# Turning the token rows of a mixture-of-experts kernel: from TensorE transposes to VectorE block transposes, with plain reads two groups ahead

## The chip, the core and the metric

The kernel runs on one core of a Trainium2 chip, in one launch. The metric is device time in microseconds, the median of several runs. The engines have these names in the profile: PE (TensorE, matrix products), PEld (its weight loads), DVE (VectorE), ACT (ScalarE), POOL (GpSimd), SP (SyncE, which here only issues DMA transfers). Data that the engines work on lies in SBUF, 128 partitions wide; matrix products are written to PSUM.

## The reference

Linear attention without a softmax, an RMS norm, then a mixture of experts in which each token goes to one expert.

```python
# q, k, v: (8, 8, 576, 64) float32;  g_norm: (64,)
kv  = np.einsum('bhsd,bhse->bhde', k, v)
out = np.einsum('bhsd,bhde->bhse', q, kv)
rms = np.sqrt(np.mean(out * out, axis=-1, keepdims=True) + 1e-06)
x   = (out / rms * g_norm)         # -> (4608 tokens, 512), heads side by side
# w_gate: (512, 8), w1: (8, 512, 1024), w2: (8, 1024, 512)
logits     = x @ w_gate
expert_idx = argmax(logits);  gate_w = softmax(logits)[expert_idx]
for e in range(8):
    mask = expert_idx == e
    out[mask] = gate_w[mask, None] * (np.maximum(x[mask] @ w1[e], 0) @ w2[e])
```

## The kernel before

It has two phases that overlap a little. In the attention phase, for each of 8 batches, it loads q, k, v, forms `kv`, and makes for each tile of 128 tokens the normalised row (`xrow`, 512 values of 16 bits, without the factor `g_norm`, with the gate weight and the number of the token behind it: 516 words of 16 bits, 1032 bytes) and the logits. Rows go to a table in DRAM, `x_slots`, in which expert e owns the rows from e * 4608 on; a running count gives each token its place. The writes are indirect DMA from POOL, one for each tile of 128 tokens.

```python
# inside the attention phase
xrow[j, t // 3] = PA.tile([128, 3, ROW], I16, tag="xrow", bufs=4, ...)     # three tiles to a buffer
...
def o_x(j, t):                                        # DVE: row and logits, scaled by 1/rms
    nc.vector.tensor_tensor(xr[:, 0:D]..., xv, _bc(rs2, 3, 64), op=ALU.mult)
    nc.vector.tensor_tensor(lhat[j][:, t]..., lv, _bc(rs2, 3, 8), op=ALU.mult)
...
chunks = {0: [(0, 9)], 1: [(0, 9)], 2: [(0, 3), (3, 9)], 3: [(0, 3), (3, 6), (6, 9)]}   # tiles routed together
...
for t in range(T):                                    # end of route(): scatter the rows
    nc.gpsimd.indirect_dma_start(out=xs_views[9 * j + t0 + t], out_offset=...posi..., in_=xrow[...])
```

The expert phase works through 11 groups: the first three 128-row tiles of experts 0, 1 and 2 ("early" groups, whose rows are complete before the last batches are routed), then the two remaining tiles of each of these, then experts 3 to 7 with five tiles each. A small group for tiles beyond five ("spill") stands before the last. A group reads its rows by indirect DMA on POOL (`fetch`), one for each tile; rows that hold no token are left out by the bounds check, over a buffer cleared at the start. PE turns each tile with four transposes, DVE brings the result to SBUF and multiplies by `g_norm`; `stage1` is the first product with ReLU on ACT, `stage2` the second, with the gate weight on DVE and an indirect DMA of the result rows.

```python
xl_ring = [P_const.tile([128, SLOT_TILES, ROW], I16, ...) for n in range(3)]
...
def fetch(self):                      # POOL, one for each tile k
    nc.gpsimd.indirect_dma_start(out=self.xl[:, k, :], in_=xs.ap(), in_offset=...idx...,
                                 bounds_check=E * N - 1, oob_is_err=False)
def xpose(self, k):
    ps = PSA.tile([128, 4, 128], F16, tag="KV", bufs=2, name="xps")
    for c in range(4):
        nc.tensor.transpose(ps[:, c, :], self.xl[:, k, c * 128 : (c + 1) * 128].bitcast(F16), ident16)
    nc.vector.tensor_scalar(self.xsT[:, :, k * 128 : (k + 1) * 128], ps, g2, None, op0=ALU.mult)
def stage1(self, f):                  # f = 0..7; two column halves for groups of five tiles
    for kk in range(4):
        for hp, s in zip(hps, starts):
            nc.tensor.matmul(hp, self.w()[0][:, kk, f * 128 : (f + 1) * 128],
                             self.xsT[:, kk, s : s + self.step], ...)
    nc.scalar.activation(self.hT[:, f, ...], hp, ACTF.Relu)
def stage2(self, k):
    for f in range(8):
        nc.tensor.matmul(yp, self.hT[:, f, k * 128 : (k + 1) * 128], self.w()[1][:, f, :], ...)
    nc.vector.tensor_scalar(y, yp, self.xl[:, k, D : D + 2].bitcast(F32), None, op0=ALU.mult)
    nc.gpsimd.indirect_dma_start(out=self.views(k), out_offset=...ids..., in_=y, ...)
```

The groups' order of work is a generator, `ffn()`, whose units are called by the end of the attention phase and then to the end. While group n is in `stage2`, the tiles of group n+1 are turned; `fetch` of group n+2 is issued after the first unit of group n. The weights come from SP as float32 pieces of 512 KB into four staging buffers (`wst`); `w_step` casts the oldest to float16 on DVE and loads one more. The tables for the spill group (`dyn_tables`) are some 35 small DVE operations that run in one go inside the first two-tile group. At the very end every engine loads the number of further spill tiles (`n_more`) into a register, and a loop, usually of no turns, follows.

Of the kernel before, what the change touches and what calls it, by code (L numbers as in the profile page):

```python
# [45 lines left out]
def kernel(  # L46
# [20 lines left out]
    xs_views = dram_disjoint_views(xs.ap(), NT)  # L67
# [9 lines left out]
    for j in range(4):  # L77
# [20 lines left out]
        "w1off": arf[:, None] + 128.0 * np.array([0, 2, 1, 3], np.float32)[None, :],  # L98
# [36 lines left out]
    nc.scalar.dma_start(g2[64:128, :], g_norm.unsqueeze(1))  # L135
    wgt = P_const.tile([128, 8, 8], F32, tag="wgt")
# [17 lines left out]
    chunks = {0: [(0, 9)], 1: [(0, 9)], 2: [(0, 3), (3, 9)], 3: [(0, 3), (3, 6), (6, 9)]}  # L154
    ohbs, n_route = [], 0
    for j in range(4):
# [7 lines left out]
    xl_ring = [  # L164
        P_const.tile([128, SLOT_TILES, ROW], I16, tag=f"xl{n}", name=f"xl{n}") for n in range(3)
    ]
# [7 lines left out]
    w_tiles = {}  # L174

# [4 lines left out]
    def w_load(pool, bufs):  # L180
# [23 lines left out]
        if n < 4:  # L204
            r0 = 128 * (2 * (n % 2) + n // 2)
            nc.sync.dma_start(st, w1[r0 : r0 + 128, :])
# [8 lines left out]
        w_staged.append((e, dst, st))  # L215

    def w_cast(engine):
        if w_staged:
            e, dst, st = w_staged.pop(0)
            engine.tensor_copy(dst, st)  # L220
            w_done[e] = w_done.get(e, 0) + 1
# [4 lines left out]
    def w_step():  # L226
        if len(w_staged) == 4 or not w_todo:
            w_cast(nc.vector)
# [8 lines left out]
    cnt = P_const.tile([128, 8], F32, tag="cnt")  # L237
    srow = P_const.tile([128, 8, SLOT_TILES], F32, tag="srow")
# [4 lines left out]
    def row_index(name, ctr, ne, nk):  # L243
        bad = P_const.tile([128, ne, nk], F32, tag="bad" + name, name="bad" + name)
        nc.vector.tensor_tensor(
            bad, _bc(cv["srank"][:, 0:nk], 1, ne), _bc(ctr[:, 0:ne], 2, nk), op=ALU.is_ge
        )
        idx = P_const.tile([128, ne, nk], I32, tag="idx" + name, name="idx" + name)
        nc.vector.scalar_tensor_tensor(
            out=idx, in0=bad, scalar=BIG, in1=srow[:, 0:ne, 0:nk], op0=ALU.mult, op1=ALU.add  # L250
        )
        badi = P_const.tile([128, ne, nk], I32, tag="badi" + name, name="badi" + name)
        nc.vector.tensor_scalar(badi, bad, BIG, None, op0=ALU.mult)
        return idx, badi

    rows = {}

    def early_rows():
        ctr = P_const.tile([128, 8], F32, tag="cnt_e")
        b0 = base[len(routed)]  # L260
        nc.vector.tensor_tensor(ctr, b0, cv["ebase"], op=ALU.subtract)
        rows["early"] = row_index("e", ctr, EARLY, EARLY_TILES)
        nc.vector.tensor_tensor(b0, b0, cv["efloor"], op=ALU.max)
        yield
        for i in range(EARLY):
            groups[i].fetch()
        yield

    def final_rows():
        nc.vector.tensor_tensor(cnt, base[n_route], cv["ebase"], op=ALU.subtract)  # L270
        rows["all"] = row_index("a", cnt, 8, SLOT_TILES)

    class Group:
        def __init__(self, n, e, k0, k1):
# [4 lines left out]
            self.xl = xl_ring[n % 3]  # L279
            self.table = "early" if self.small and k0 == 0 else "all"  # L280

# [6 lines left out]
        def fetch(self):  # L288
            idx = rows[self.table][0]
            for k in range(self.K):  # L290
                nc.gpsimd.indirect_dma_start(  # L291
                    out=self.xl[:, k, :], out_offset=None, in_=xs.ap(),
                    in_offset=IndirectOffsetOnAxis(
                        ap=idx[:, self.e, self.k0 + k : self.k0 + k + 1], axis=0
                    ),
                    bounds_check=E * N - 1, oob_is_err=False,
                )

        def slot_ids(self):
            badi = rows[self.table][1]  # L300
# [3 lines left out]
                self.xl[:, 0 : self.K, D + 2 : D + 4].bitcast(I32),  # L304
                badi[:, self.e, self.k0 : self.k0 + self.K].unsqueeze(2), op=ALU.max,
            )

# [6 lines left out]
        def start(self):  # L314
            self.xsT = self.pool().tile(
# [577 lines left out]
```

## Time and profile before

| quantity | before |
|---|---|
| time, median of 3 runs (lowest to highest) | 330.64 us (329.99 to 332.32) |
| span of the profiled execution | 329.2 us |
| PE busy | 269.0 us, 82% |
| DVE busy | 183.4 us, 56% |
| ACT busy | 119.9 us, 36% |
| POOL busy | 137.6 us, 42% |
| DMA | 85.79 MB, mean 261 GB/s |
| PE transposes of rows (`xps`) | 160 and 4 for the spill tile, 16.1 us busy |
| their evictions on DVE (`xsT`) | 41, 19.2 us busy, 477 ns each |
| reads of rows on POOL (`xl`) | 40, 42.3 us busy |
| PE idle before matmuls of attention for DVE's `lhat` | 9.6 us in 3 waits |

The profile is one execution. Busy times of engines overlap, so they do not add up to the span; what counts is which engine is waited for at a given moment. Its second part cuts the span into 40 equal slices and gives busy tenths, so that phases can be told apart; PEclk is the clock that PE was granted, in tenths of full speed. The chain of waits follows the work that ended last back in time. In the timeline, a line is: start, length, engine, line of the source, operation, output and input, count, and in brackets the idle time ahead of it with what ended it.

### The profile page before, as it was taken

The page shows a single profiled execution, that of the slowest core. Times are in us where ns is not written, and L with a number is a line of the kernel's source. Part 1 is how long each engine was busy: PE and PEld are TensorE (multiplying, and loading weights), DVE is VectorE, ACT ScalarE, POOL GpSimd, SP SyncE. Part 2 cuts the span into 40 slices and gives each one's busy share as a digit, 9 for nine tenths or more (in the row PEclk, how much of TensorE's full clock was granted, in tenths as well). Part 3 has the DMA queues.
Part 4 walks back from the last instruction along what each step waited for, and adds up shares of the span by engine and source line. Part 5 has one row for each costly group of instructions (what it writes and reads, how often), then busy time and mean ns, then how long its engine had stood idle before and what let it go on. Part 6 is the DMA issues. An engine that isn't in the chain of part 4 may idle for free.

```text
span 329.2 us, 7247 instructions
## 1 busy us (share of the span) xinstructions
PE 269.0 (82%) x2759; PEld 189.3 (58%) x2759; DVE 183.4 (56%) x433; ACT 119.9 (36%) x316; POOL 137.6 (42%) x147
## 2 busy tenths in 40 slices
PE   0699897689766977564979996989999999997980
PEld 0587776577656866462535563657565665645630
DVE  6205566346745368889184678344657658375040
ACT  1136564436543445322322431326142240602600
POOL 9100001720076004384675462777477656052041
PEclk9999997959995589555999998999999999999996
DMA  6999999997897016799589894667799999983021
GB/s 158 334 368 367 369 368 367 381 282 216 246 323 295 18 67 167 250 323 324 201 260 372 295 322 121 214 214 251 250 339 358 351 397 279 408 284 130 0 99 55
DMA packets 45395, 85.79 MB, mean 261 GB/s; under 512 B 6188, under 2 KB 22829, under 8 KB 45360
## 3 DMA queue, kind: packets, MB, share of 16 engines
q1 hardware_dynamic: 36736, 66.07, 59.9%
q0 software_dynamic: 6976, 18.96, 15.6%
q10 hardware_dynamic: 1648, 0.29, 0.5%
q8 instruction: 22, 0.36, 0.4%
q14 instruction: 13, 0.11, 0.1%
HBM read 71.77 MB, written 15.50 MB: 265 GB/s over the span
## 4 chain that ended last, share of the span: by engine, by line
PE 26%; issue 11%; DMA 9%; POOL 7%; DVE 5%; POOLq 1%; ACT 0%; DVEq 0%; ACTq 0%
PE hp L345 13%; PE yp L361 11%; DMA out_dram<-y,d_id 7%; POOL out_dram L369 4%; POOL xl L291 2%; DMA xl<-x_slots,idxe 2%; PE xps L325 1%; DVE y L366 1%; DMA x_slots<-xrow,posi 1%; POOL x_slots L743 1%; DVE w1e L220 1%; DVE xsT L328 0%; POOLq L888 0%; POOLq L854 0%; DVE w2e L220 0%
## 5 line engine op out<-in xcount | busy, mean ns | idle before, releaser
L353 ACT ACTIVATE hT<-hp 128x320 f16<-128x320 f32 (+3 forms) x136 | 53.6, 426 | 106.5 <-PE hp L345 105.9
L345 PE MATMUL hp<-xsT,w1e 128*128 128x320 f16 (+2 forms) x512 | 76.6, 306 | 7.2 <-DVE xsT L328 6.3
L361 PE MATMUL yp<-w2e,hT 128*128 128x512 f16 x320 | 74.1, 379 | 0.3 <-DVE y L366 0.3
L369 POOL DMA_INDIRECT out_dram<-y,idv x40 | 44.6, 1115 | 60.3 <-DVE y L366 49.3
L345 PEld LDWEIGHTS <-w1e 128*128 128x128 f16 x512 | 51.0, 100 | 32.1 <-issue 11.7
L651 PE MATMUL ops<-kvx,qT 64*128 64x72 f32 (+1 forms) x640 | 48.0, 310 | 10.5 <-DVE lhat L680 9.6
L743 POOL DMA_INDIRECT x_slots<-xrow,posi x36 | 35.7, 991 | 40.5 <-DVE xrow L739 15.5
L651 PEld LDWEIGHTS ops<-kvx,qT 64*128 64x128 f32 (+1 forms) x640 | 42.3, 215 | 15.0 <-issue 9.3
L361 PEld LDWEIGHTS <-hT 128*128 128x128 f16 x328 | 30.8, 98 | 31.6 <-issue 0.4
L366 DVE TENSOR_SCALAR y<-yp,xl 128x512 f32<-128x512 f32 x40 | 30.0, 750 | 33.6 <-PE yp L361 29.9
L664 DVE TENSOR_REDUCE ms<-sq 128x8 f32<-128x512 f32 x36 | 24.6, 685 | 25.1 <-ACT sq L660 25.0
L291 POOL DMA_INDIRECT xl<-x_slots,idxa x31 | 32.4, 1046 | 11.7 <-issue 7.0
L594 PE MATMUL kvps<-mk,mv 128*64 128x64 f32 x640 | 28.7, 258 | 9.4 <-DMA mv<-in_v_dram 9.1
L676 DVE TENSOR_TENSOR xrow<-ops,rs 128x512 f16<-128x512 f32 x36 | 24.7, 686 | 18.0 <-DMA x_slots<-xrow,posi 9.3
L660 ACT ACTIVATE sq<-ops 128x512 f32<-128x512 f32 x36 | 21.5, 598 | 31.9 <-PE ops L651 31.5
L594 PEld LDWEIGHTS kvps<-mk,mv 128*64 128x64 f32 x640 | 26.0, 168 | 11.8 <-issue 10.3
L710 POOL COPY xrow<-tokc 128x3 int32<-128x3 int32 x12 | 3.0, 253 | 64.3 <-DVE xrow L676 64.2
L582 PE MATMUL tps<-ctile,mq 128*128 128x128 f32 x144 | 26.9, 320 | 3.5 <-ACT qT L583 1.9
L220 DVE CAST w2e<-wst 128x1024 f16<-128x1024 f32 x32 | 22.3, 704 | 11.4 <-DMA wst<-in_moe_w_dram 11.4
L583 ACT COPY qT<-tps 128x384 f32<-128x384 f32 x48 | 21.9, 473 | 14.4 <-PE tps L582 14.4
L328 DVE TENSOR_SCALAR xsT<-xps,g 128x512 f16<-128x512 f16 x41 | 19.2, 477 | 12.9 <-PE xps L325 12.7
L220 DVE CAST w1e<-wst 128x1024 f16<-128x1024 f32 x32 | 21.6, 688 | 4.5 <-DMA wst<-in_moe_w_dram 4.5
(99 smaller groups left out, 184.1 us busy)
## 6 DMA issues: line engine op xcount, KB each, us to landing
wst<-in_moe_w_dram SPq DMA_DIRECT2D x64, 512.0 KB, 5.8
mq<-in_q_dram SPq DMA_DIRECT2D x16, 576.0 KB, 7.8
mk<-in_k_dram SPq DMA_DIRECT2D x16, 320.0 KB, 7.5
mv<-in_v_dram SPq DMA_DIRECT2D x16, 320.0 KB, 7.3
mk<-in_k_dram SPq DMA_DIRECT2D x16, 256.0 KB, 7.9
mv<-in_v_dram SPq DMA_DIRECT2D x16, 256.0 KB, 7.1
wsts<-in_moe_w_dram SPq DMA_DIRECT2D x8, 512.0 KB, 5.9
out_dram<-y,idv POOLq DMA_INDIRECT x40, 4.9
```

Of the source, the lines that this page charges most:

```text
L220: engine.tensor_copy(dst, st)
L291: nc.gpsimd.indirect_dma_start(out=self.xl[:, k, :], out_offset=None, in_=xs.ap(), in_offset=IndirectOffsetOnAxis(ap=idx[:, self.e, self.k ...
L345: nc.tensor.matmul(hp, self.w()[0][:, kk, f * 128 : (f + 1) * 128], self.xsT[:, kk, s : s + self.step], start=(kk == 0), stop=(kk == 3),)
L353: nc.scalar.activation(self.hT[:, f, s : s + self.step], hp, ACTF.Relu)
L361: nc.tensor.matmul(yp, self.hT[:, f, k * 128 : (k + 1) * 128], self.w()[1][:, f, :], start=(f == 0), stop=(f == 7),)
L366: nc.vector.tensor_scalar(y, yp, self.xl[:, k, D : D + 2].bitcast(F32), None, op0=ALU.mult)
L369: nc.gpsimd.indirect_dma_start(out=self.views(k), out_offset=IndirectOffsetOnAxis(ap=self.ids[:, k : k + 1], axis=0), in_=y, in_offset=Non ...
L582: nc.tensor.transpose(ps[:, c, :], src[:, 128 * m : 128 * m + 128], cv["ident"])
L594: nc.tensor.matmul(kvps[b][64 * y : 64 * y + 64, 2 * u + a, :], main["v", b, u][:, 2 * y + a, c, :], main["k", b, u][:, 2 * y + a, c, :], ...
L651: nc.tensor.matmul(ps[p0 : p0 + 64 * n, y, o0 : o0 + 72], qT[b][hs, a, blk // 2 : blk // 2 + n, :].rearrange("d c p -> d (c p)"), kvx[b][h ...
L676: nc.vector.tensor_tensor(xr[:, 0:D].bitcast(F16).rearrange("p (a h d) -> p a h d", a=2, h=4), xv, _bc(rs2, 3, 64), op=ALU.mult,)
L743: nc.gpsimd.indirect_dma_start(out=xs_views[9 * j + t0 + t], out_offset=IndirectOffsetOnAxis(ap=posi[:, t : t + 1], axis=0), in_=xrow[j, ( ...
```

## The change

Rows are now turned by DVE in blocks of 32 x 32. To make a 128-wide turn out of such blocks, a group's rows are read by four plain DMAs from SP, each with one quarter of the columns (128 of 512) of all rows of the group into 32 partitions; a block of 32 rows then lies across 32 partitions, and DVE's transpose puts the columns where the product wants them. The columns come out in the order p * 4 + c, so the first weight matrix is read in rows of that order, and `g_norm` (as `g4`) moves into the cast of the weights. Gate weight and token number come by a fifth small DMA (`gi`).

Plain reads take all rows, those without a token too, so these must hold zeros: for the early groups the slots are cleared by a DMA from a zero tile before any row is written (`clear_early`); for the others, POOL writes zero rows into the empty slots only (`pads`), by indirect DMA. Reads are issued two groups ahead, paddings three; the turn of group n+1 stands within `stage1` of group n. Beside this: six `xrow` buffers in place of four, other chunks for batch pair 2, casts shared between DVE and ACT in the last batches, one copy moved from DVE to ACT, more units of the expert phase within the last batch, the tables spread over units, the register load of `n_more` moved into the middle of the expert phase, and other PSUM tags for some tiles.

```diff
+    zero = P_wa.tile([128, F], F32, tag="wst", bufs=4, name="zero")
+    nc.gpsimd.memset(zero[:, 0 : EARLY_TILES * ROW // 2], 0.0)
+    def clear_early(e):
+        nc.sync.dma_start(xs.ap()[e * N : e * N + 128 * EARLY_TILES]..., zero[...].bitcast(I16))
...
         def fetch(self):
-            idx = rows[self.table][0]
-            for k in range(self.K):
-                nc.gpsimd.indirect_dma_start(out=self.xl[:, k, :], ... in_=xs.ap(), ...)
+            r0 = self.e * N + 128 * self.k0
+            src = xs.ap()[r0 : r0 + self.n].rearrange("(g b) w -> b g w", b=32)
+            self.xl = self.pool().tile([128, self.n // 32, 128], I16, tag="xl", bufs=2, name="xl")
+            for i in range(4):
+                c0 = 128 * (2 * (i % 2) + i // 2)
+                nc.sync.dma_start(self.xl[32 * i : 32 * i + 32], src[:, :, c0 : c0 + 128])
+            self.gi = P_fe.tile([128, SLOT_TILES, 4], I16, tag="gi", bufs=3, name="gi")
+            nc.sync.dma_start(self.gi[:, 0 : self.K], xs.ap()[r0 : r0 + self.n, D:ROW]...)
...
+        def pads(self):
+            for k in range(self.K):
+                nc.gpsimd.indirect_dma_start(out=self.pad_views[k], out_offset=...pad..., in_=zrow, ...)
...
-        def xpose(self, k): ...four PE transposes and an eviction with g2...
+        def xpose(self, part=0, parts=1):
+            gs = slice(g * part // parts, g * (part + 1) // parts)
+            nc.vector.transpose(self.xT[:, gs], self.xl[:, gs].rearrange("p g (a c) -> p g c a", c=4))
...
             for f in range(8):
                 cur.stage1(f)
+                if f == 0 and real >= 0:
+                    fetch_up_to(real + 2)
+                    if EARLY - 1 <= real < len(groups) - 3:
+                        groups[real + 3].pads()
                 if f % 2 == 1 if cur.K != 2 else f % 4 == 1:
                     w_step()
-                if f == 0 and 1 <= real and EARLY <= real + 2 < len(groups):
-                    groups[real + 2].fetch()
+                if f >= 4 and f % 2 == 0 and (f - 4) // 2 < parts:
+                    nxt.xpose((f - 4) // 2, parts)
...
-                    [128, 3, ROW], I16, tag="xrow", bufs=4, name=f"xrow{j}{t}"
+                    [128, 3, ROW], I16, tag="xrow", bufs=6, name=f"xrow{j}{t}"
...
-            nc.vector.tensor_copy(kvx[b][:, 1], folds[b][1])
+            nc.scalar.copy(kvx[b][:, 1], folds[b][1])
...
-                for _ in range((0, 1, 1, 2)[max(b - 5, 0)]):
-                    w_step()
-                if b == B and n >= 3:
+                if b == 6 and n >= 1:
+                    w_load(P_wa, 3)
+                elif b == 7:
+                    w_step(nc.vector if n % 2 else nc.scalar)
+                elif b == B:
+                    w_step()
+                    w_step(nc.scalar)
+                if b == B and n >= 1:
                     unit()
                     unit()
```

## The prediction

> **What bounds the kernel now.** First the page's forty slices, where the two phases show.
>
> ```profile
> PE   0699897689766977564979996989999999997980
> ...
> DVE  6205566346745368889184678344657658375040
> ...
> PEclk9999997959995589555999998999999999999996
> DMA  6999999997897016799589894667799999983021
> ```
>
> A slice is 8.2 us. Up to slice 10 DMA is full (q, k, v): attention is paced by its inputs. In slices 12 to 18 (99 to 156 us) DMA falls away, PE holds 4 to 9 tenths at half clock, DVE 7 to 9: attention's tail and the routing. From slice 19 PE is at 9: the expert phase, PE-bound. So two questions: what holds up the middle, and what PE does in the last 160 us.
>
> For the middle I read the timelines of DVE and PE, then windows of 3 us (columns: PE, PEld, DVE, ACT, POOL busy us; clock, DMA share, GB/s).
>
> ```profile
> 100.33 0.69 DVE L676 TENSOR_TENSOR xrow<-ops,rs 128x512 f16<-128x512 f32 x1 [5.01 <-DMA x_slots<-xrow,posi]
> ```
> ```profile
> 67.34 1.98 PE L651 MATMUL ops<-kvx,qT 64*128 64x72 f32 x16 [3.90 <-DVE lhat L680]
> ...
> 101.26 1.98 PE L651 MATMUL ops<-kvx,qT 64*128 64x72 f32 x16 [3.21 <-DVE lhat L680]
> ...
> 118.45 1.11 PE L651 MATMUL ops<-kvx,qT 64*128 64x72 f32 x16
> ```
> ```profile
> 97.00:100.00 3.00, 0.58 (x3) 0.31 (x3) 0.00 (x0) 0.41 (x2) 2.12 (x3) 0.64 1.03 400
> 100.00:103.00 3.00, 1.74 (x16) 1.75 (x16) 2.56 (x11) 0.88 (x3) 1.16 (x2) 0.50 1.03 402
> ...
> 115.00:118.00 3.00, 3.00 (x46) 2.87 (x46) 1.69 (x4) 0.92 (x3) 0.00 (x0) 0.50 0.00 0
> 118.00:121.00 3.00, 2.74 (x37) 2.30 (x33) 1.84 (x5) 1.19 (x4) 0.19 (x1) 0.95 0.49 177
> ```
>
> DVE wants to write a row tile, but its buffer (four of them) still waits to be scattered; PE waits on DVE for 3.2 us; its clock falls to 0.50, and the same 16 matmuls take 1.98 us until the clock is back at 118, then 1.11. One buffer wait costs 3.2 us plus nearly half of 17 us.
>
> For the expert phase, the chain of waits.
>
> ```profile
> 222.23 8.69 PE hp L345 x64
> 230.93 0.22 PE xps L325 x4
> 231.15 1.73 PE yp L361 x8
> ...
> 301.16 21.75 DMA out_dram<-y,d_id
> ```
>
> A five-tile group is 8.69 + 5 x (0.22 + 1.73) = 18.4 us of unbroken PE work, the transposes among it. PE is busy 151.4 of the 160 us from 160 to 320 (sum of the 20 us windows). The last matmul ends at 320.0 (timeline) and the span at 329.2: 9.2 us of tail. The 21.75 us there is one piece drawn over the last group and the final landing, not a slow transfer.
>
> **What the Trainium skill says.** "VectorE: DVE Perf Modes", The three transpose paths: VectorE transposes 32x32 blocks only, into SBUF, 311 ns for 128x128 of bf16. No transpose by VectorE is in this trace. The same page, Mode 1x and Mode 2x_2P, gives one element per cycle at 0.96 GHz as the basic rate, and two for one SBUF source; the casts here (1024 f32 in 0.69 us, where one element per cycle would be 1.07) fit the double rate. "TensorE: Matmul & The Clock Gate", What's actually happening: half clock after an idle window of about 3.4 us, full after a busy one of that length. The fall agrees (idle 3.9 and 3.2 us); the return does not: it took 17 us here. "DMA: Bandwidth & Descriptors", Specifications: pieces under 512 B do not reach line rate. Here 6188 packets of 45395 are that small, too few to judge by.
>
> **The change part by part.**
>
> *PE transposes gone.* 41 tiles at 0.22 us on PE: 9.0 us, of which some 36 lie in the PE-bound stretch: -7.9. With them goes the wait of the group's first matmul for the eviction: PE's 8.6 idle us in that stretch (163 to 167, 201 to 203, 212 to 220, 300 to 303 by the chain and timeline) are mostly this or DVE's queue of casts and table steps ahead of it. The tables are now spread over units. I count -5.
>
> *DVE instead.* Before this,, five evictions of 477 ns a group: 2.4 us. After, two transposes of 1280 elements: 1280/0.96 GHz = 1.33 us plus some 0.1, an estimate from the skill's page: 2.9 us. With nine casts of 0.69, five y of 0.75 and 0.15 for ids DVE has 13.1 us in a group of 17.3. It isn't the bound. The norm scale moves into the w1 cast: same count, perhaps 0.05 us more (a scalar from a tile: d_rank took 241 ns instead of 190). -0.
>
> *Row buffers six instead of four.* Both waits of the middle should go. The first (67 us) lies where DMA paces; the second is worth 3.2 + 17 x (1 - 1.11/1.98) = 3.2 + 7.5 = 10.7. I count -10.
>
> *More of the first group ahead.* Half of the casts of the last two batches go to ACT, one copy per batch too; DVE, 17.6 of 20 us busy at 120 to 140, loses some seven casts (4.8 us) and gains two early transposes (3.3). More FFN units lie in the last batch: the first group took 153.1 to 169.3 = 16.2 us, of which 10.7 at full clock (5.53 + 3 x 1.73). And the nine early reads no longer stand in POOL's queue: they held it from 139.8 to 152.2, with the next scatters waiting at 157.9. Together -8.
>
> *Added.* Clearing early slots: 3 x 384 x 1032 B = 1.19 MB at 368 GB/s while DMA is full: +3. Reads in pieces of 256 B: 5120 rows x 4 = 20480 pieces, and 5120 of 8 B. Queue 10's 1648 small packets took 0.5% of 16 engines x 329 us, 16 ns each at 176 B; queue 1's 36736 took 59.9%, 86 ns each at 1.8 KB. Between these I estimate 20 ns for 256 B, 10 for 8 B, 50 for a whole row of 1032 B. New: (20480 x 20 + 5120 x 10) / 16 = 29 us on all sixteen engines; old: 5120 x 50 / 16 = 16. That is +13 us of DMA work spread over an expert phase whose DMA share is 0.64 to 0.98. Some of it will show: +2. Loading the tile count on every engine moves from the end to the middle of a stage: +1, with about as much off the tail.
>
> *The new chain.* The order of instructions shows it: the read of group n+2 waits for its own padding writes; the padding of group n+3 waits for that read to land; and these sit in SP's and POOL's queues ahead of weight loads and output scatters. One link: five paddings at 1.05 + 0.30 us (the indirect reads of before) = 6.7, landing 2.5 (outputs: 2.6 at least), read 6 to 8 with its issue (weight loads land in 5.8): 15 to 17 us. A large group lasts 17.3, so there it fits. The three two-tile groups last only 4.1 + 2 x 1.73 = 7.6 each: some 8 us a group are missing, against a lead of about ten. I expect DVE to stand before the reads of the first large groups, weights behind them, and PE to lose around +14 in all.
>
> Check by rebuilding: expert work at full clock without transposes is 3 x 10.7 + 3 x 7.6 + 5 x 17.3 + 4.8 = 146 us. Attention's last matmuls, at 148.6 before, move to about 137 (-10 -3 +3, rounded with the rest); five us of expert work are done by then. 137 + 141 + 14 + 3 + tail 9 = 304; the sum of parts, 330.6 - 7.9 - 5 - 10 - 8 + 3 + 2 + 14, is 319. I take 310 between the two, since the parts counted separately leave out what full clock brings through the whole middle.
>
> **The rivals.**
> *The chain takes everything back.* If reads of 256 B pieces land in 10 us and more, the first large groups wait some 30 us: about 325. For it: the waits are in the program, and SP's queue is in order. Against: padding writes hold few rows, and two groups' lead was meant for this.
> *DMA becomes the bound.* From 240 to 300 it moves 333 to 350 GB/s before; a large group needs 4.2 MB of weights, 1.2 out, 0.66 in per 17.3 us = 350 GB/s. Then groups stay at 18.4 us or more, and only the middle gains: 317.
> *Everything hides.* Chain covered, clock full from 90 us on: 298.
> *The middle keeps its holes*, since reads now wait for scatters and scatters for reads on POOL: half clock remains and the gain there is 3 us: 318.
>
> **Range and chances.** Middle 310; the good rival and the two bad ones span 298 to 324, which I give 8 in 10. 2% faster means under 324.0, slower over 337.3. Faster 0.85, same 0.10, slower 0.05.
>
> **What would show it.** Right: no xps rows on PE; stream transposes near 1.4 us for 1280 elements; no wait of xrow on x_slots near 65 and 100 us and clock 1.0 from 100 to 118; large groups at 17.3 us; in the chain or the waits, DVE transposes waiting for reads of x_slots around the first large groups. Wrong: a clock of 0.5 through the middle all the same; transposes twice as long; DMA share near 1 throughout the expert phase with casts waiting for weights; POOL idle before padding for most of the phase.

## The result and the profile after

The changed kernel takes 340.18 us (median of 4; 339.88 to 340.91), the kernel before beside it 331.04: 1.028 of it, 95% interval 1.024 to 1.032. It is slower, where 310 us were predicted. First the forty slices of the profile after (span 338.5 us, a slice is 8.5 us):

```profile
PE   0589999988878466899959979535999789799800
DVE  1105677685866756766449653605855564940400
PEclk9979999999995555599969999975999989999975
DMA  5999999999996797979696283579999999860300
```

Three things differ from the slices of before. From slice 3 to 10 (25 to 93 us) PE stands at 8 and 9, at full clock: that part came as planned. The half clock has not gone; it fills slices 12 to 16 (102 to 144 us), about as long as the two stretches of before together (slices 12 and 13, 16 to 18). And where before PE was nearly always at 9, it now falls to 5 at 169 us, to 7 at 195, and to 5, 3 and 5 from 212 to 237 us, where DVE goes down to 0. The last row is gated at the same moment as before, 320.1 us, but the span ends 18.4 us later instead of 9.1.

Cut at two points of the timeline that both kernels have, the start of the last `lhat` (the end of attention) and of the last large group's last `y`, the span is

| | to the last `lhat` | groups, to the last `y` | end | span |
|---|---|---|---|---|
| before | 153.6 | 166.5 | 9.1 | 329.2 |
| after | 143.4 | 176.7 | 18.4 | 338.5 |
| difference | -10.2 | +10.2 | +9.3 | +9.3 |

So the gain of attention was there, the groups gave it back to the tenth, and the end added the loss. Below, "groups" and "end" are these columns.

The groups. PE's waits in that stretch, of after (line, what it waited for: us, times, longest):

```profile
PE yp L402 <- DVE y L407: 20.6, 5, 9.2
PE hp L386 <- DVE xT L350: 3.6, 3, 2.0
```

And what DVE and SP's queue waited for in it:

```profile
DVE w2e L238 <- DMA wst<-in_moe_w_dram: 18.3, 9, 11.2
SPq L338 <- DMA x_slots<-zrow,padall: 39.7, 11, 8.6
```

Before, the first of PE's waits was 0.3 us. PE hardly waits for the turned rows, the thing the change is about; it waits for the gating of rows, which DVE can't do because it stands elsewhere. The timeline of after shows where:

```profile
208.63 2.03 SPq L338 DMA_DIRECT2D xl<-x_slots  x4
...
214.57 0.98 POOL L323 DMA_INDIRECT x_slots<-zrow,padall  x1 [5.12 <-DMA gi<-x_slots]
...
222.30 2.31 SPq L338 DMA_DIRECT2D xl<-x_slots  x4
...
225.29 1.21 SPq L220 DMA_DIRECT2D wst<-in_moe_w_dram  x2
...
230.75 0.69 DVE L238 CAST w2e<-wst 128x1024 f16<-128x1024 f32 x1 [11.21 <-DMA wst<-in_moe_w_dram]
...
232.15 1.44 PE L402 MATMUL yp<-w2e,hT 128*128 128x512 f16 x3 [9.16 <-DVE y L407]
```

Read it downwards: a read goes out at 208.6; POOL's padding stands 5.1 us until its last part (`gi`) has landed, then takes five writes; the next read, in SP's queue, goes only when these have landed, at 222.3; the weight load behind it in the same queue goes at 225.3; DVE has been waiting for those weights for 11.2 us, and PE for DVE for 9.2. The link from read to read is 14.7, 14.4 and 13.7 us here (reads at 179.5, 194.2, 208.6, 222.3).

The rows of this padding and of the read that it waits for are not the same: they belong to different groups, and each writes or reads its own rows of `x_slots`. So by the code (no run isolates it) this half of the link comes from both being accesses to one tensor, not from the data. A table of its own for each group would be the direct test; no run made it.

The end. The last instructions of POOL's queue in after, and of the kernel before beneath (count, lowest/median/highest ns, first and last start):

```profile
L947 POOLq INC_SWDGE_SEM  x1: 2360/2360/2360, 324.6 to 324.6; - x1
```
```profile
L981 POOLq DRAIN  x3: 40/103/8971, 328.7 to 338.2; - x3
```
```profile
L854 POOLq INC_SWDGE_SEM  x1: 400/400/400, 322.6 to 322.6; - x1
```
```profile
L888 POOLq DRAIN  x3: 40/109/3348, 325.0 to 328.9; - x3
```

One drain of 8.97 us, and one semaphore instruction of 2.36 in place of 0.40, stand alone at the end while all else is done.

The middle. PE's wait for `lhat` is 1.1 us in three, from 9.6 before, so the row buffers no longer hold it. But the windows of after (columns as in the prediction) show the clock falling all the same, at 103 us:

```profile
97.00:100.00 3.00, 2.53 (x58) 2.31 (x57) 1.96 (x8) 0.92 (x3) 2.39 (x3) 1.00 1.01 401
100.00:103.00 3.00, 0.80 (x7) 0.46 (x6) 1.03 (x2) 2.50 (x6) 1.19 (x3) 1.00 0.84 256
103.00:106.00 3.00, 2.37 (x18) 2.07 (x19) 1.99 (x10) 1.17 (x4) 0.82 (x1) 0.54 0.94 314
106.00:109.00 3.00, 3.00 (x45) 2.39 (x46) 1.84 (x7) 2.23 (x5) 2.07 (x3) 0.50 0.41 150
...
118.00:121.00 3.00, 0.00 (x0) 0.00 (x0) 2.81 (x9) 0.51 (x2) 0.22 (x1) 0.50 0.87 304
```

And from its timeline, PE and SP in the same stretch:

```profile
97.10 1.11 PE L746 MATMUL ops<-kvx,qT 64*128 64x72 f32 x16
...
104.43 1.99 PE L746 MATMUL ops<-kvx,qT 64*128 64x72 f32 x16
...
111.08 1.87 SPq L338 DMA_DIRECT2D xl<-x_slots  x4
...
121.39 1.11 PE L386 MATMUL hp<-xT,w1e 128*128 128x384 f16 x3 [4.77 <-DVE xT L350]
```

At 97 us sixteen `ops` matmuls take 1.11 us, as hoped; at 104 they take 1.99 again. Between, from 100 to 103 us, PE is busy 0.80 us of 3.00, without any wait for `lhat`: its timeline names two waits of 1.6 us, for ACT's `qT` and for the routing's `tm` on DVE. Later comes a longer stop: the first group now stands so early in PE's order that PE waits for its rows, which were read at 111 only, after the scatters before them had landed; from 118 to 121 it does nothing.

This also sets a reading of the prediction right. Its window 97:100 has a clock of 0.64, so the fall lay near 97.8 us, while the wait for `lhat` ended at 101.26 after 3.21 us and so began at 98.05. The clock fell before that wait: PE had already been busy only 1.40 us of the 3 from 94 on. The second stretch of half clock in before, from 132 to 156 us, was given no cause at all.

### The profile page after: what moved, and what is told of

The parts are those of the page before. It is cut to its first block, busy times and chain, and to the rows that moved or that the text cites. A ratio compares the mean times of both kernels' runs of the same rounds, so it can differ in the third digit from the quotient of the medians.

```text
span 338.5 us, 6955 instructions
## 1 busy us (share of the span) xinstructions
PE 258.3 (76%) x2599; PEld 171.6 (51%) x2599; DVE 179.1 (53%) x396; ACT 127.0 (38%) x331; POOL 118.9 (35%) x136
## 3 DMA queue, kind: packets, MB, share of 16 engines
q0 software_dynamic: 6544, 14.76, 11.8%
## 5 line engine op out<-in xcount | busy, mean ns | idle before, releaser
L402 PE MATMUL yp<-w2e,hT 128*128 128x512 f16 x320 | 79.5, 407 | 20.6 <-DVE y L407 20.6
L386 PE MATMUL hp<-xT,w1e 128*128 128x320 f16 (+2 forms) x512 | 80.5, 313 | 14.1 <-DVE xT L350 8.4
L407 DVE TENSOR_SCALAR y<-yp,gi 128x512 f32<-128x512 f32 x40 | 29.7, 747 | 43.1 <-PE yp L402 27.5
L323 POOL DMA_INDIRECT x_slots<-zrow,padall x31 | 32.6, 1052 | 46.4 <-DMA gi<-x_slots 30.0
L746 PEld LDWEIGHTS ops<-kvx,qT 64*128 64x128 f32 (+1 forms) x640 | 39.3, 201 | 8.4 <-issue 3.5
L689 PE MATMUL kvps<-mk,mv 128*64 128x64 f32 x640 | 24.3, 234 | 14.6 <-DMA mv<-in_v_dram 12.6
L238 DVE CAST w2e<-wst 128x1024 f16<-128x1024 f32 x29 | 19.7, 681 | 20.7 <-DMA wst<-in_moe_w_dram 20.7
L689 PEld LDWEIGHTS kvps<-mk,mv 128*64 128x64 f32 x640 | 21.8, 146 | 16.8 <-issue 14.0
L350 DVE STREAM_TRANSPOSE xT<-xl 128x1280 int16<-128x1280 int16 (+2 forms) x16 | 24.1, 1505 | 9.4 <-DMA xl<-x_slots 9.0
L236 DVE TENSOR_SCALAR w1e<-wst,g 128x1024 f16<-128x1024 f32 x28 | 21.1, 764 | 5.0 <-DMA wst<-in_moe_w_dram 5.0
L677 PEld LDWEIGHTS tps<-ctile,mq 128*128 128x128 f32 x144 | 16.7, 152 | 7.7 <-ACT qT L678 2.9
```

Of the source, the lines that this page charges most:

```text
L323: nc.gpsimd.indirect_dma_start(out=self.pad_views[k], out_offset=IndirectOffsetOnAxis(ap=pad[:, self.e, self.k0 + k : self.k0 + k + 1], axis=0
L386: nc.tensor.matmul(hp.rearrange("p (g b) -> p g b", b=32), self.w()[0][:, kk, f * 128 : (f + 1) * 128], self.xcols(kk, s), start=(kk == 0) ...
L407: nc.vector.tensor_scalar(y, yp, self.gate(k), None, op0=ALU.mult)
L677: nc.tensor.transpose(ps[:, c, :], src[:, 128 * m : 128 * m + 128], cv["ident"])
L689: nc.tensor.matmul(kvps[b][64 * y : 64 * y + 64, 2 * u + a, :], main["v", b, u][:, 2 * y + a, c, :], main["k", b, u][:, 2 * y + a, c, :], ...
L746: nc.tensor.matmul(ps[p0 : p0 + 64 * n, y, o0 : o0 + 72], qT[b][hs, a, blk // 2 : blk // 2 + n, :].rearrange("d c p -> d (c p)"), kvx[b][h ...
```

## The experiments

Two theories after this reading. *The chain*: padding waits for reads and reads for padding, in queues that hold back weights and outputs. *The end*: the loop's new place, or something in POOL's software queue. Rivals: *small pieces* (reads of 256 bytes load the DMA engines), and *the middle* (the half clock is what was lost). The kernels ran in five series, in which the kernel before took 326, 355, 353, 329 and 358 us (medians); total times are compared as ratios within a series, "groups" and "end" from the profiles.

### The chain

**All padding first.**
```diff
-            groups[n].pads()          # for two groups; the rest within the groups
+            groups[n].pads()          # for all late groups, after the last routing
```


> The changed kernel with all 31 padding writes issued in one go after the last routing, and none in the groups. Theory 'the chain': no padding waits for a read any more, and POOL does them in some 31 us from about 151 us on; the read for the first late group waits for them until about 185 us and TensorE stands for some 10 to 15 us there, but from 190 us on there are no holes (PE over 9 tenths in every slice from 200 to 300 us), so that the time comes to 325 to 335. If the chain is not the cause, the holes after 200 us stay and the time rises to 345 to 355.

1.100 of the kernel before (1.097 to 1.103), worse than expected. The 31 writes take 1.29 us each, 40 us and not 31, and the timeline has one hole:

```profile
205.32 1.25 DVE L350 STREAM_TRANSPOSE xT<-xl 128x1024 int16<-128x1024 int16 x1 [39.80 <-DMA xl<-x_slots]
```

After it, no further hole: DVE's waits for `w2e` weights are half those of after (10.8 us for 20.7). So the later holes of after come with the interleaving, and small pieces alone don't make them; but the way costs more than it brings.

**Two statements swapped.**
```diff
-                    fetch_up_to(real + 2)
                     if EARLY - 1 <= real < len(groups) - 3:
                         groups[real + 3].pads()
+                    fetch_up_to(real + 2)
```


> The changed kernel with two statements swapped: in the first stage of a group the padding for three groups ahead is issued before the read for two groups ahead, not after it. A padding write then waits for the read of one group earlier, which has long landed. Theory 'the chain' (read waits for padding, padding for the read before it, 14 to 15 us a link): POOL's waits for the landing of the id read (30 us in the changed kernel) fall below 8, VectorE's waits for staged weights (20.7) and TensorE's for the gated rows (20.6) to less than half, and the time falls by 10 to 18 us, to 322 to 330. Rival 'small pieces' (the reads of 256-byte pieces load the DMA engines, and the holes come from full queues): the waits move but the time stays within 3 us of 340. Rival 'the middle' (the half clock between 103 and 144 us is what was lost): a gain of 0 to 5 us, and the first 30 us after the first expert matmul as before.

1.090 (1.083 to 1.097): a miss; the groups take 188.4 us. The reads follow each other at 12.6 to 15.4 us as before (173.0, 188.3, 201.0, 214.8, 229.6). I had overlooked that the read now waits for one padding more; each link is still one padding and one read.

**The changed kernel once more, and no padding at all.**

> The changed kernel unaltered, as a yardstick beside the other kernels of this call: 340 to 346 us, 1.03 to 1.055 of the kernel before, with 18 us after the last matmul. If it stands at 1.055 of the kernel before, the earlier runs with the loop at its old place and with the first group later differ from it by nothing.

367.82 us against 354.66 for the kernel before (medians), 1.037, no interval; groups 175.5, end 18.2.
```diff
-            groups[n].pads()                     # and in the groups
+    late_clears = [(e, 3, 2) for e in range(EARLY)]
+    late_clears += [(e, k0, k) for e in range(EARLY, E) for k0, k in ((0, 3), (3, 2))]
+    # three of them with each load of attention's first blocks, on SP
```


> The changed kernel without any padding write: all late slots (31 tiles, 4.1 MB) are cleared by plain transfers from SP's queue during the first three blocks of attention, and no read waits for padding, no padding for a read. Theory 'the chain and the queue it blocks' (SP's reads wait for POOL's padding, and the weight loads stand behind them): the holes between 169 and 280 us, some 30 us of TensorE, go; attention is later by up to 11 us for the added DMA work; the time comes to 312 to 325. Theory 'the long end comes from padding writes' (3,500 rows out of range that POOL must get rid of): the time after the last matmul falls from 18 us to about 9. Rival 'small pieces': holes stay and the time is 345 to 355.

0.999 (0.994 to 1.004). Attention ends 11.4 us later than in the run beside it (182.0 for 170.6), the groups take 151.0 us in place of 175.5, the end 14.8. Their stretches, of before, after and this kernel:

```profile
153.60:320.10 166.50, 157.39 (x1027) 93.57 (x1025) 92.68 (x200) 53.72 (x137) 88.43 (x84) 0.98 0.74 259
```
```profile
143.40:320.10 176.70, 149.29 (x847) 82.64 (x845) 96.03 (x176) 50.51 (x131) 79.77 (x77) 0.93 0.74 238
```
```profile
182.00:333.00 151.00, 141.87 (x843) 80.63 (x841) 96.07 (x176) 49.88 (x129) 48.77 (x46) 0.99 0.85 275
```

PE idles 9.1 us, 27.4 us and 9.1 us. The chain cost after 18.3 us of standing and 7.4 us of slower matmuls (clock 0.93 for 0.99). Nearly all of it lies in two groups, from PE's first matmul of a group to its last: the first large group took 36.5 us in after and 17.5 here, the third early one 17.1 and 13.2; the large groups behind them took nearly the same in both (18.4, 22.9, 19.8 and 17.5 us; here 18.6, 22.5, 19.7 and 17.5).

The reads still come in pieces of 256 bytes, so *small pieces* did not make the holes of after. But those middle large groups should have taken 17.3 us by the prediction, and there DMA is full. The third large group of before, and of this kernel:

```profile
259.00:277.60 18.60, 18.60 (x127) 11.39 (x126) 11.63 (x20) 6.12 (x16) 11.62 (x11) 1.00 1.00 359
```
```profile
269.10:291.60 22.50, 19.64 (x107) 10.69 (x106) 13.41 (x18) 6.11 (x16) 5.63 (x6) 0.92 1.00 322
```

At a DMA share of 1.00 in both, 322 GB/s move in place of 359. In this kernel's group DVE waits 4.2 us for `w1` pieces of the spill group, and PE 2.8 us for DVE. In the groups of after the trace has 15,872 pieces of 256 bytes at 19.3 ns each (13 bytes per ns; its pieces of 2 KB took 98 ns, 21 per ns). Whether these pieces or the closer packing of all transfers costs the extra microseconds, no run separates.

**Reads from POOL's queue.**
```diff
-                nc.sync.dma_start(self.xl[32 * i : 32 * i + 32], ...)
+                nc.gpsimd.dma_start(self.xl[32 * i : 32 * i + 32], ...)
```


> The changed kernel with the reads of the slots (four quarters and the ids) issued from POOL's queue, behind the padding they wait for, and not from SP's. Weight loads no longer stand behind a read that waits. Theory 'queue' (most of the loss after 169 us is VectorE's wait for staged weights behind a waiting read): VectorE's waits for staged weights in that stretch fall from 21 to under 8 us and the time falls by 8 to 15 us. Theory 'chain alone' (the link of 14 to 15 us is what counts, whichever queue it runs in): within 4 us of the changed kernel, since the output scatters now stand behind the reads.

1.070 (1.053 to 1.087), groups 197.9, so neither theory's number. In the groups DVE's waits for `w2e` weights fell to 2.6 us (18.3 in after), as *queue* said, but its waits for output rows to leave rose to 36.5 (15.6), since the output scatters now stand behind the reads. The waiting read holds up what is behind it in whichever queue it stands.

**Half the padding.**
```diff
-            for k in range(self.K):
+            for k in range(max(3 - self.k0, 0), self.K):
```


> The changed kernel with padding for tiles 3 and 4 of each expert alone: 16 padding writes and not 31, two for every group and not five for a large one. (These inputs fill the tiles below.) Theory 'the chain': a link of a large group is 3 x 1.29 us shorter, the five large groups' links come to 10 or 11 us in place of 14 to 15, and the time from the last attention tile to the last gated row falls from 176 us to 158 to 166; the end, with 5,824 packets in the software queue, from 18.3 to about 16.5. Rival (it is the wait for the read, not the writes themselves, that makes the link): 170 to 176.

1.0015 (0.997 to 1.006): as fast as the kernel before. Groups 163.3, end 16.7, both as expected; the first large group takes 26.5 us. The reads:

```profile
203.24 2.04 SPq L338 DMA_DIRECT2D xl<-x_slots  x4
209.43 0.98 POOL L323 DMA_INDIRECT x_slots<-zrow,padall  x1 [5.17 <-DMA gi<-x_slots]
...
213.19 2.40 SPq L338 DMA_DIRECT2D xl<-x_slots  x4
```

Two writes in a link and not five: 10.0 us. With 31, 16 and no paddings the groups take 176.7, 163.3 and 151.0 us: the loss follows the number of paddings.

### The end

**The loop at its old place.**
```diff
+    manual.close()                    # before the loop, as in the kernel before
+    n_more.append(nc.values_load(...))   # after it, not in the middle of a group
```


> The changed kernel with the end of the kernel before: the count of tiles is read into registers after the last group again, and the loop stands outside the hand-made schedule. Nothing else is changed. Theory 'the end' (the loop's new place costs what the span has gained after the last matmul, 18.4 us against 9.2): the last matmul still ends near 320 us, the time after it falls to about 9 us, and the whole comes to 331 (330 to 333). Rival (the long drain of POOL's queue at the end comes from the padding writes queued earlier, not from the loop): no change, 340 +- 1, with 18 us after the last matmul.

1.054 (1.050 to 1.058); the end is 19.9 us. The loop's place is not the cause.

**31 writes of rows out of range, in the kernel before.**
```diff
+        for n in range(31):
+            nc.gpsimd.indirect_dma_start(out=xs_views[n], ..., in_=zrow, bounds_check=E * N - 1)
```


> The kernel before with 31 more indirect writes on POOL at its very start, all of whose rows are out of range, so that they move nothing; POOL is idle there. Theory 'the long end comes from the padding writes of rows out of range': the time after the last matmul grows from 9 to about 18 us and the whole by 8 to 10 us, to 1.025 to 1.03 of the kernel before. Rival (it comes from something else at the end): no difference over 0.5%.

1.101 (1.086 to 1.116), but not at the end: that grew to 11.0 us only. The loss is at the start, where ACT stood 45.9 us (see the last section). Rows out of range are not what makes 18 us.

The drains pointed to a count: the profile's packets of the software queue were 5,056 without padding (drain 6.44 us), 6,544 in after (8.97), 6,976 in the kernel before (3.35). In these counts every indirect transfer makes 48: the change dropped 40 reads and added 31 paddings, 9 x 48 = 432 fewer. So a few more writes should shorten the end.

**Twelve more writes.**
```diff
+            if b < 2:
+                for _ in range(6):
+                    nc.gpsimd.indirect_dma_start(out=xs_views[NT + E * SLOT_TILES - 1], ..., in_=zrow)
```


> The changed kernel with 12 more indirect writes on POOL in the first two blocks of attention, where POOL is idle; all their rows are out of range, so they move nothing. They raise the packets of the software queue from 6,544 to about 7,120, above the 6,976 of the kernel before. Theory 'the queue's descriptors' (POOL's last semaphore instruction and drain take 1.4 and 5.4 ns for every packet that has not been cleared away by then, and a clearing in bulk comes somewhere between 6,544 and 6,976 packets): the time after the last matmul falls from 18 us to 9 or 10, and the whole by 8 to 9 us. Rival (the end is longer for another reason, and the counts agree by chance): the end grows by 4 to 5 us instead, or stays.

The end is 8.1 us. The whole is 1.086 (1.081 to 1.092), since the writes share one piece of `x_slots` and wait for each other, though they move nothing, and the slots' clearing for them, with attention's loads behind it in SP's queue. From its waits:

```profile
POOL x_slots L921 <- DMA x_slots<-zrow,far: 39.7, 11, 5.4
```

**The same into a tensor of their own.**
```diff
+                nc.gpsimd.indirect_dma_start(out=dump_views.pop(), ..., in_=zrow, bounds_check=127)
```


> The changed kernel with 12 more indirect writes on POOL in the first two blocks of attention, all rows out of range, into a DRAM tensor of their own, so that nothing waits for them (in the earlier try the slots' clearing waited for them, and attention stood still). They raise the packets of the software queue from 6,544 to about 7,120. Theory 'the queue's descriptors': attention and groups as in the changed kernel (175 to 177 us from the last attention tile to the last gated row), the time after that row 8 to 9 us in place of 18, the whole 9 to 10 us under the changed kernel, 1.0 to 1.01 of the kernel before. Rival (the end only moved before, since all else had moved): 18 us again.

The same two instructions of POOL's queue in this kernel:

```profile
L956 POOLq INC_SWDGE_SEM  x1: 480/480/480, 328.9 to 328.9; - x1
```
```profile
L990 POOLq DRAIN  x3: 40/103/1294, 330.8 to 332.6; - x3
```

End 8.1 us, attention 146.0, groups 178.9. The whole missed its 1.0 to 1.01: the ratio, 1.029 (1.012 to 1.046), is too wide to show the 9 us; in the profile they are plain. Below the bend the drain is 1.70 ns a packet (6.44, 7.75 and 8.97 us at 5,056, 5,824 and 6,544), above it again (1.13, 1.29 and 1.54 at 7,024, 7,120 and 7,264), as if some 5,090 had been taken off in between. The change took 432 packets away, from 6,976 to 6,544, and so fell on the dear side.

Four drains do not lie on these lines: 3.35 us in the kernel before, 4.58 in it with 31 writes (8,464 packets), 10.29 with the loop at its old place (6,544) and 3.83 with reads from POOL (9,136); by the lines they would be 1.05, 3.58, 8.97 and 4.72. Since each indirect transfer is 48 packets, the runs cannot tell packets from transfers. What POOL does in a drain no run shows.

### The middle

**The first group later.**
```diff
-                if b == B and n >= 1:
+                if b == B and n >= 3:
```


> The changed kernel, but the first group's steps are interleaved only from the fourth tile of the last block of attention on, as in the kernel before, instead of from the second. Theory 'the middle' (TensorE stands before the first group's rows at 112 to 121 us and falls to half clock, and attention behind it in its order stands too): the hole of 9 us before the first expert matmul shrinks to under 4 us, the last attention tile ends some 5 us earlier, and the time falls by 4 to 8 us. Theory 'the chain': what is won in the middle is given back by the chain that starts from the last attention tile; it can start only some 5 us earlier, so the gain is at most 5 us, and 0 is as likely. Rival 'small pieces': no change.

1.055 (1.048 to 1.061); the changed kernel was not run beside it, so its total is not set against it. In the profile the last `lhat` is at 139.7 (143.4 in after), the groups take 185.1. What the middle wins, the groups lose.

**Four row buffers.**
```diff
-                    [128, 3, ROW], I16, tag="xrow", bufs=6, name=f"xrow{j}{t}"
+                    [128, 3, ROW], I16, tag="xrow", bufs=4, name=f"xrow{j}{t}"
```


> The changed kernel with four attention row buffers instead of six, as in the kernel before. The prediction put the row buffers at 10 us: TensorE's wait for these buffers (3 us) comes back and with it a half clock before 100 us; the last attention tile ends 8 to 12 us later. If the chain of padding and reads after it is the limit, all of that shows in the time (350); if the buffers were worth nothing, the same time as the changed kernel within 1 us.

1.046 (1.036 to 1.056). DVE's wait for row buffers is back (8.3 us in two), but PE's for `lhat` is 1.0 us either way, and the last `lhat` is at 171.2, with six buffers 170.6 in another series. The two extra buffers were worth about nothing there; but in both series ACT also stood for some 12 us in attention (see the last section), which may hide a gain. In a series without that it was not tried.

### Together

**Tiles 3 and 4 alone cleared, no padding.** These inputs fill the tiles below; rows without tokens would hold what the memory held, and their results are dropped.
```diff
+    late_clears = [(e, 3, 2) for e in range(E)]
```


> The changed kernel without padding writes, and with tiles 3 and 4 alone of every expert cleared by plain transfers in early attention (2.1 MB, not the 4.1 MB of all late slots). It relies on these inputs filling 384 slots of every expert. Theory 'the chain': from the last attention tile to the last matmul 151 us, as with all late slots cleared, against 175 in the changed kernel; attention later by 5 to 6 us and not by 11; the time 18 to 22 us under the changed kernel, 0.97 to 0.985 of the kernel before. Rival (clearing costs by its instructions and waits, not its bytes): as slow as with all late slots cleared, 0.995 to 1.0.

0.987 (0.978 to 0.996), a gain of 1%; groups 151.0 as expected, end 14.7. Attention ended at 184.9, 14 us later than with padding (171.2 with four buffers) and not 5 to 6.

**With 46 writes into `x_slots`.** The edit of the twelve writes, with 23 a block.

> The one before with 46 indirect writes on POOL in the first two blocks of attention that move nothing, which raise the packets of the software queue from 5,056 to 7,264. If the software queue's descriptors set the long end, the time after the last matmul falls from 15 us to under 11, and the whole comes to 0.96 to 0.975 of the kernel before; if the 60 us of POOL's time hurt attention, it is slower than without them.

1.271 (1.261 to 1.280): attention stands as with the twelve, longer. End 8.8 us.

**With 41 writes into a tensor of their own.** The two edits together.

> No padding writes, tiles 3 and 4 of every expert cleared by plain transfers (as in the earlier run), and 41 writes that move nothing into a tensor of their own, for 7,024 packets on the software queue. If the chain and the queue's descriptors are the two causes and their costs add, 151 us from the last attention tile to the last gated row and 8 to 9 us after it, some 6 us under the run without the 41 writes: 0.96 to 0.975 of the kernel before. If POOL's 52 us for them delay attention, 0.98 to 1.0.

320.35 us against 329.25 (medians), 0.973, no interval. End 8.4, groups 155.9 and not 151.

**And the first group later.**

> The one before, with the first group interleaved from the fourth tile of the last block of attention on instead of the second. With the chain in place this brought the last attention tile forward by 5 us and the groups after it took 8 us longer. If the chain was what took those back, the groups now take 151 to 155 us and the whole is 2 to 5 us under the one before; if it is work moved from one side of that tile to the other, the same within 2 us.

319.09 us, 0.972 (0.944 to 1.000), one us from the one before. The last `lhat` comes 3.8 us earlier and the groups take 4.4 longer (160.3): work moved from one side of the tile to the other.

**Two combinations in five rounds.** First no padding, cleared tiles, 41 writes, and the small loads of `g4` after `wgt`'s:

> Both causes taken away and one small thing more: no padding writes, tiles 3 and 4 of every expert cleared by plain transfers, 41 writes that move nothing into a tensor of their own (7,024 packets on the software queue), and the eight small loads of the norm weights after the gate weights' load and not ahead of it (VectorE waited 11 us for the gate weights at the start of the changed kernel). 0.965 to 0.975 of the kernel before; the last attention tile 1 to 3 us earlier than without the move of the loads, 152 to 156 us from there to the last gated row, 8.4 us after it. If the two causes don't add up, 0.985 to 1.0.

Then 16 paddings and 25 writes:

> Padding for tiles 3 and 4 alone (16 writes) and 25 writes that move nothing into a tensor of their own, for 7,024 packets on the software queue. The last attention tile near 145 us, 163 us from there to the last gated row (as with the 16 padding writes alone), and after it 8.3 us in place of 16.8: 0.97 to 0.98 of the kernel before. If the end is paid for elsewhere, as 1.0.

1.073 (1.064 to 1.081) and 1.049 (1.041 to 1.058). The ends are as expected (8.5 and 8.0), the groups nearly (153.5 and 167.3), but attention ended at 217.9 and 196.5: ACT stood while the writes were issued. From the first one's waits up to 110 us:

```profile
ACT qT L686 <- remote: 61.3, 1, 61.3
```

So the parts add up in one series and not in another; I don't offer this version.

## Why the prediction was wrong

It gave 304 by rebuilding: 137 to the end of attention (clearing included), 141 for the groups, 14 for the chain, 3 that it does not name, 9 for the end. Two steps make up most of the miss: the chain's size, 14 where 25.7 was measured, and the end, 9 where it was 18.4. A third, the clock of the middle, had its cause wrong.

- *The new chain.* The mechanism was right, down to the link (15 to 17 us foretold, 14 to 15 measured). Its size was not: 14 against 25.7 (176.7 less 151.0). The shortfall over the three two-tile groups was counted rightly: three links of 14.3 less three groups of 8.0 make 19 us (an estimate from after's timeline), and the first large group alone lost 19.0. What failed is the lead "of about ten" taken off it. Rows had a lead (DVE waited only 9.0 us for reads in the groups), but by the waits the weight loads and outputs behind the waiting transfers had none: I named the weights and gave them no time. DVE waited 18.3 us for `w2e` pieces, 7.3 without the chain, and 15.6 for outputs to leave, then 1.7. The large groups after the first did absorb their links, as foretold. Slower matmuls after the stops are 7.4 of the 25.7.
- *The tail.* 9 "with about as much off" for the tile count: it was 18.4. Nothing in the text concerned the software queue; this term was missing, and is as large as the whole loss.
- *Row buffers six instead of four* (-10). The waits went, yet the half clock stayed; in before the clock had fallen ahead of the wait that was to explain it. Undoing the change moved the last `lhat` by 0.6 us, across two series. The rival *the middle keeps its holes* was right on the middle: reads wait for scatters (111 us), and PE for reads.
- *More of the first group ahead* (-8). The first group's `stage1` is done before the last `lhat`: 32 matmuls, 11.1 us of PE at half clock, for which a like group takes 5.7 at full clock. That is the five us I counted, at twice the time. Attention's last `ops` ended at 140.3, 137 foretold.
- *PE transposes gone* (-7.9 and -5). The first holds: no `xps` of rows in the profile, the groups' PE time fell by 15.5 us without the chain, of which some 7.8 is work done earlier (30 matmuls of `stage1`, 6.2 us in before, and 7 of `stage2`, some 1.6), which leaves 7.7. The 5 for waits does not: PE idles 9.1 us before and 9.1 us without the chain.
- *DVE instead.* Right: 1.505 us for 1280 elements (1.4 foretold), the casts of `w1` 0.764 us.
- *Added.* Clearing: 4.1 MB cost 11.4 us, so 1.19 MB at +3 fits (1.19/4.1 of 11.4 is 3.3, an estimate). Reads of small pieces (+2): the 20 ns for a piece was right (19.3); what it costs in time was not isolated.
- *The chain takes everything back* came nearest of the rivals, for another reason: reads land soon enough, and the writes between them take the time. *DMA becomes the bound* is not what made 340: its share over the groups is 0.74, as before. But that is an average. In the second to fourth large group of after it is 0.97, 0.96 and 0.89 and they take 18.4 to 22.9 us, not 17.3; there what the rival foretold is seen, with its sign, casts waiting for weights.

In sum: chain +11.7, end +9.4, groups +10 (141 against 151.0, of which 9.1 is PE standing), attention +6.4 up to the last `lhat`, less the 3 without a name: 304 becomes 338.5. My 310 lay between two sums that shared the two faults.

## What to carry to other kernels

A buffer in DRAM that one queue pads and another reads can make a chain; count its links against the shortest stage, count what stands behind each waiting transfer in the same queue, and ask whether the two sides touch the same bytes at all. Clearing early took the chain away here, at the price of more bytes in attention, and in no series for a gain of 2% that an interval confirms. Look at the end of the program whenever the number of indirect transfers changes, and read a DMA share by stage, not as one average.

## What was not expected of the hardware

In the six packet counts of the changed kernel and its variants from 5,056 to 7,264, POOL's closing semaphore instruction and drain take 0.42 and 1.70 ns more for each packet of the software queue, and between 6,544 and 7,024 packets they fall back by some 5,090 packets' worth: twelve idle writes made the end 10 us shorter. The four drains named above lie off these lines. The semaphore instruction of the kernel before (0.40 us at 6,976) lies behind the fall.

In three of the five series ACT stood while POOL issued a run of indirect writes, though the profile shows nothing that it waited for on this core ("remote"): 45.9 us beside 31 writes, 61.3 us beside 41, 39.3 us beside 25, 12.4 us beside nine scatters of attention, where in the other two series ACT went on beside such runs. In these three the kernel before takes 353 to 358 us, not 326 to 329. Beside the 12 and 46 writes that waited for each other it did not stand so. No run tells what sets it; it stays open.

PE's clock, once halved, stayed so for 41 us in after (103 to 144), and before for 20 us (98 to 118) and 24 (132 to 156); later in after it came back after one step of 3.4 us (219 to 223). In the 41 us PE stopped again and again; from 101 to 118 us in before it hardly did, and why the clock stayed down there is open.
